# Later fetches of the raw channel weights, some scalings given to VectorE, and joined k-v products, in a fused attention and mixer kernel

## The chip, the cores and the metric

The kernel runs on one core of one Trainium2 chip. The metric is the device time of one execution in microseconds; of several runs the median counts. Engines are called by the names of the profile: PE is TensorE's matrix multiply, PEld its weight load, DVE is VectorE, ACT is ScalarE, POOL is GpSimd, SP is SyncE, which here only issues DMAs.

## The reference

Eight batches of 576 tokens go through a linear attention of 8 heads of 64, and then through an MLP mixer.

```python
kv = np.einsum('bhsd,bhse->bhde', k, v)
out = np.einsum('bhsd,bhde->bhse', q, kv)
rms = np.sqrt(np.mean(out * out, axis=-1, keepdims=True) + 1e-06)
x = out / rms * g_norm            # then (B, S, H*D): 8 x 576 x 512
h = np.maximum(xt @ w_tok1, 0.0) @ w_tok2       # xt = x with tokens last
u = x + h.transpose(0, 2, 1)
h2 = np.maximum(u @ w_ch1, 0.0) @ w_ch2
out = u + h2
```

w_tok1 is 576 x 256, w_tok2 256 x 576, w_ch1 512 x 1536, w_ch2 1536 x 512. The four weights arrive as float64, q, k and v as float32.

## The kernel before, in words

**Pairs and stages.** Batches are taken two at a time, as four pairs. The program has an attention for each pair, and a token mixing for each pair, which turns the pair's x into u and writes it to DRAM (`u_dram`). They are played against each other: a stage holds the attention of one pair and the token mixing of the pair before. So there are five stages: "start" (attention of pair 0), "middle" (attention of pair 1, mixing of pair 0), two "steady" stages (attention of pairs 2 and 3, mixing of pairs 1 and 2), and "last" (mixing of pair 3). Then follows the channel mixing, three quarters of the span: group 0 by `channel1_once` and `channel2_once` (L619, L681), groups 1 to 8 by `channel1` and `channel2`, which are not touched.

**The order is written by hand.** Each stage is a list of strings of step names, and `play` (L1047) emits the steps in that order; `keep` holds every engine to it, so each engine executes its own steps in this order, and waits at a step until its inputs and its buffer are there. In the names, the first digit after the letters is mostly a chunk, c, and the second a half or a tile, t:

- `kv00`, `kv01`, `kv10`, `kv11`: the products of k and v of side 0 or 1 (a batch of the pair), for one half of the heads: 20 matmuls, which the profile counts as 40 (`kv`, L319). PE takes every fp32 matmul here as two instructions. `e00` and so on copy the result from PSUM (ps_kv, two buffers) to SBUF (kvp); outside the start this is ACT's.
- `a0` to `a3`, `a4`: the attend products of q and kvp for one chunk of tokens (a4: the remainder of both sides), into two PSUM banks ps_o, of which there are only two (`attend`, L359; `attend_rem`, L373). After each come two `g` (x = ps_o times the gain, DVE, L399) and two `q` (squares, ACT, L403), which free the banks. a0 and a1 read the q of side 0, a2 and a3 that of side 1, a4 both.
- `t` sums the squares (DVE, L420), `m`, `r`, `i` make the inverse root for a group of chunks (DVE, ACT, DVE).
- `s` scales a tile of x, 128 x 512, by the inverse root on ACT, as 8 instructions, one for each head (`scale`, L448); `p` does it whole on POOL (`scale_pool`, L455).
- `h00` to `h11` and `hr`: the first token product, of 512 columns, into PSUM ps_h; hr also makes h1 by four relus on ACT. `u0` to `u8`: the second token product, into ps_u; u then adds x on DVE, or, where a seed `z` has put x into the bank before (ACT, `z2`, `z4`, `z6`), ACT copies it out. u writes its tiles to `u_dram` by POOL's queue.
- `l00` and so on fetch k and v of the next pair, `lq0` and `lq1` its q; all on SP's queue. A q buffer is free when the attends of its side are done: there are two.

**Rounding the channel weights.** The float64 weights are brought to float32 block by block: `block` (L180) gives a fetch (SP, into one of four raw buffers), a scale (two ACT instructions, L154 and L157), a clamp, a shift and an addition of 16-bit limbs (DVE, L160, L164, L169), which frees the raw buffer. Five blocks of token weights are worked off in the start by name (`w`). The fourteen channel blocks, 0 to 7 of w_ch1 (786 KB each) and 8 to 13 of w_ch2 (1049 KB, two DMAs each), come from `stream` (L1029): an iterator of single steps. A number in a stage's list takes as many steps from it. The fetches of blocks 0 to 3 stand in the lists as `f0` to `f3`; from then on the stream itself fetches block n + 4 with the shift of block n. What is left is woven into "last", with the four sums of w_ch1 blocks that the channel mixing needs (`mix_ch1`), the transposes of group 0 (`c0` to `c3`: `turn_blocks`, `fetch_t`, `fetch_u`) and, as `c4`, the sums of its uT.

Of the kernel before, what the change touches and what calls it, by code (L numbers as in the profile page):

```python
# [20 lines left out]
def kernel(  # L21
# [32 lines left out]
    nc = tc.nc  # L54
    P = 128
    B, S, DM = k.shape
    D = g_norm.shape[0]
# [7 lines left out]
    HP = H // 2  # L65
# [41 lines left out]
    def do(f, *a, **kw):  # L107
        return lambda: f(*a, **kw)
# [4 lines left out]
    keep = tc.keep_in_program_order  # L113
# [189 lines left out]
    X = {}  # L303
# [5 lines left out]
    def attention(pair, groups):  # L309
# [131 lines left out]
        def inv_of(c, t):  # L441

            inv = stats_of(c)[2]
            if whole:
                return inv[:, t].rearrange("p (k h) o -> p k h o", h=2)
            return inv[:, :, ts(t, HP)].rearrange("p h k o -> p k h o")

        def scale(c, t):  # L448
            x = X[pair, c][:, t].rearrange("p (k h d) -> p k h d", h=2, d=D)
            inv = inv_of(c, t)  # L450
            for k in range(HP):
                for h in range(2):
                    keep(nc.scalar.activation(x[:, k, h], x[:, k, h], AF.Copy, scale=inv[:, k, h]))  # L453

        def scale_pool(c, t):  # L455
            x = X[pair, c][:, t].rearrange("p (k h d) -> p k h d", h=2, d=D)
            keep(nc.gpsimd.tensor_mul(x, x, inv_of(c, t).to_broadcast([P, HP, 2, D])))

        steps = {}
# [5 lines left out]
        for c in range(5):  # L465
            if whole:
                steps |= {f"a{c}{t}": do(attend_tile, c, t) if c < 4 else attend_tile_rem
                          for t in range(parts(c))}
            else:
                steps[f"a{c}"] = do(attend, c) if c < 4 else attend_rem  # L470
            for h in range(parts(c)):
                steps |= {f"{n}{c}{h}": do(f, c, h) for n, f in zip("gqt", (gain, square, total))}
            for t in range(1 if c == 4 else 2):
                steps |= {f"{n}{c}{t}": do(f, c, t) for n, f in zip("sp", (scale, scale_pool))}
        for g in groups:
            steps |= {f"m{g[0]}": do(mean, g), f"r{g[0]}": do(sqrt, g), f"i{g[0]}": do(invert, g)}
        return steps
# [81 lines left out]
    blocks, blocks_dram = {}, {}  # L559
# [466 lines left out]
                fill[done]()  # L1026
                done += 1

    def stream(blocks, ahead=4):  # L1029

        def all_of(*fs):
            return do(lambda: [f() for f in fs])

        steps = [blocks[0][1]]
        for n in range(len(blocks)):
            first = list(blocks[n][2:])
            if n + 1 < len(blocks):  # L1040
                first[0] = all_of(first[0], blocks[n + 1][1])
            if n + ahead < len(blocks):
                first[1] = all_of(first[1], blocks[n + ahead][0])
            steps += first
        return iter(steps)

    def play(lines, after={}, **stages):  # L1047

        for name in " ".join(lines).split():
            if name.isdigit():
                for _ in range(int(name)):
                    next(stages["rounding"], lambda: None)()
            elif name[0] == "-":
                stages["before"][name[1:]]()
            else:
                next(stages[s][name] for s in ("attention", "mixing", "more")
                     if name in stages.get(s, ()))()
# [26 lines left out]
    for block in tok1[2:] + tok2:  # L1086
# [5 lines left out]


    start = [
        "kv00 e00 l00 j14 w01 w11 w02 w03 w04 w12 w13 w14", "kv01 j10 e01 l01 f0",
        "a00 g00 q00", "a01 g01 q01 t00", "a10 g10 q10 t01 m0 r0", "a11 g11 q11 t10 i0 p00 p01",
        "kv10 j6 t11 m1 r1 e10 i1 s10 p11", "kv11 j2 e11", "h000 h001 h002 h003", "a20 g20 q20", "a21 g21 q21 t20",
        "h010 t21 m2 r2", "a30 g30 q30 i2 p20", "a31 g31 q31 t30", "h011 t31 m3 r3 p21", "a40 i3 p30 g40 q40 p31",
        "h012 h013 t40 m4 r4 w21 i4 s40 lq0 l10 l11"]
    middle = [  # L1100
        "kv00 e00 w31 w22 w23 w24", "h10 f1 -lq1 w32 w33 w34", "kv01 e01 w41 w42",
        "h11 f2 w43 w44", "hr l00 f3", "a0 q00 g01 q01 g00 t00 t01", "u0 z2 1", "u1 l01 1",
        "a1 q10 g11 q11 g10 t10 t11 m0 r0", "u2 i0", "kv10 e10 z4 s00", "u3 1 s01", "kv11 e11",
        "u4 1 z6", "a2 q20 g21 q21 g20 s10", "u5 t20 t21 1", "a4 q40 g41 q41 g40 lq0", "u6 t40 t41 1 l10",
        "a3 q30 g31 q31 g30 lq1 s11", "u7 t30 t31 m2 r2 1 i2 p20 p21 s30", "u8 1 l11 s31"]

    def steady(n0, n1):
        return [
            "kv00 e00 1 -s40", "h00 1", "kv01 e01 1", "h01 1", f"a0 q00 g01 q01 g00 l00 {n0}",
            "h10 t00 t01 1", "h11 l01 2", "hr 1 z2", "a1 q10 g11 q11 g10 1", "kv10 e10 t10 t11 m0 r0",  # L1110
            "u0 i0 1", "kv11 e11", "u1 1 s00 l10", "u2 z4", "a2 q20 g21 q21 g20", "u3 s01 t20 t21",
            "u4 z6 1 l11", "a4 q40 g41 q41 g40 lq0", "u5 s10 t40 t41 1", "a3 q30 g31 q31 g30 lq1",
            "u6 s11 t30 t31 m2 r2 i2 p20 p21 s30", f"u7 1 s31 {n1}", "u8 1"]

    attentions = [attention(0, ((0,), (1,), (2,), (3,), (4,)))]
    attentions += [attention(p, ((0, 1), (2, 3, 4))) for p in range(1, B // 2)]

    mixings = [token_mixing(p, (2, 4, 6)) for p in range(B // 2 - 1)]
    mixings.append(token_mixing(B // 2 - 1, range(2, 9), (0, 1)))
    more = {f"w{n}{k}": f for n, b in enumerate(tok1 + tok2) for k, f in enumerate(b)}  # L1120
    more |= {f"f{n}": b[0] for n, b in enumerate(channel)}
    rounding = stream(channel)

    def keep_warm(n):

        o = ps["h"].tile([P, DM], F32, name="ps_j", tag="h")
        for _ in range(n):
# [4 lines left out]
    play(middle, attention=attentions[1], mixing=mixings[0], before=attentions[0],  # L1132
         more=more, rounding=rounding)
    for n in range(1, B // 2 - 1):
        play(steady(*((1, 1), (0, 0))[n - 1]), attention=attentions[n + 1], mixing=mixings[n], before=attentions[n],
             rounding=rounding)


    left.close()
# [4 lines left out]
    first = ExitStack()  # L1144
# [7 lines left out]
    def turn(i):  # L1152
# [4 lines left out]
            fetch_u(0, i // 2)  # L1157

    last = [
        "h00 c0 2 -s40 2", "h01 c1 2", "h10 c2 2", "h11 c3 2", "hr z2 1", "u0 z3 1", "u1 z4 1", "u2 z5",  # L1160
        "u3 z6 1", "u4 z7 1", "u5 z8 1", "u6 1", "u7 c4", "u8"]
    more = {f"c{i}": do(turn, i) for i in range(J)}
    more[f"c{J}"] = lambda: [f() for f in outer_u(0)]
# [28 lines left out]
    n = len(sums1) // 3  # L1192
# [61 lines left out]
```

## Time and profile before

| | us |
|---|---|
| median of 3 runs | 807.58 (806.7 to 808.29) |
| the profiled execution, its time | 809.79 |
| its span, first to last instruction | 808.0 |
| PE busy | 789.6 (98%) |
| DVE busy | 638.8 (79%) |
| ACT busy | 316.1 (39%) |
| POOL busy | 92.7 (11%) |
| HBM read / written | 137.79 / 36.57 MB |

A PE that is busy in the page isn't at its peak: the ends of matmuls are modelled, and waits shorter than a matmul's pipeline hide in them. Times between the starts of weight loads or of groups of matmuls tell more. The mean granted clock of the core was 0.998. The profile's times are of one execution and are counted from its first instruction.

### The profile page before, as it was taken

What the parts mean: (1) busy time and instruction counts of PE and PEld (TensorE: products, weight loads), DVE (VectorE), ACT (ScalarE), POOL (GpSimd) and SP (SyncE); (2) the same over time, 40 slices, a digit from 0 to 9 for tenths busy, and PEclk for the clock granted to TensorE, in tenths of its full rate; (3) what the DMA queues carried; (4) which work ended last, traced back from release to release, by engine and by line L of the source; (5) the groups of instructions that cost most, each with busy time, mean ns of one, the idle gap of its engine ahead of it and who ended that gap; (6) DMA issues with size and microseconds to landing.
All of it is one profiled execution on the core that took longest, in us unless ns stands there. A gap on an engine that the chain in (4) does not pass through costs nothing.

```text
span 808.0 us, 17626 instructions
## 1 busy us (share of the span) xinstructions
PE 789.6 (98%) x7008; PEld 694.4 (86%) x7008; DVE 638.8 (79%) x1251; ACT 316.1 (39%) x857; POOL 92.7 (11%) x95
## 2 busy tenths in 40 slices
PE   6999998999999999999999999999999999999997
PEld 6655544544888899999999999999999999999997
DVE  2667577584786978978987997997897898799687
ACT  2377787664120134234234234332423423423331
POOL 1211111021000021012003003001101200300300
PEclk9999999999999999999999999999999999999999
DMA  9999999328258477468457648738736845763642
GB/s 291 321 358 338 343 331 364 119 92 261 102 175 296 170 243 232 135 214 271 146 203 238 197 156 257 231 118 270 256 121 218 265 158 192 240 199 125 216 147 82
DMA packets 95041, 175.50 MB, mean 217 GB/s; under 512 B 7024, under 2 KB 54128, under 8 KB 94960
## 3 DMA queue, kind: packets, MB, share of 16 engines
q1 hardware_dynamic: 90656, 163.21, 62.4%
q0 software_dynamic: 2624, 9.44, 3.0%
q10 hardware_dynamic: 1680, 1.74, 0.7%
q8 instruction: 55, 0.90, 0.4%
q14 instruction: 26, 0.21, 0.1%
HBM read 137.79 MB, written 36.57 MB: 216 GB/s over the span
## 4 chain that ended last, share of the span: by engine, by line
PE 84%; DVE 5%; DMA 5%; ACT 4%; SPq 1%; issue 1%; DVEq 0%; ACTq 0%
PE ps_a L128 36%; PE ps_b L128 18%; PE ps_c L128 9%; PE ps_u L128 6%; PE ps_h L128 6%; PE ps_v L128 3%; PE ps_w L128 2%; PE ps_o L128 2%; ACT x L453 2%; DMA qT<-in_q_dram 1%; DMA raw<-in_moe_w_tok_dram 1%; DMA xt<-u_dram 1%; PE ps_kv L128 1%; SPq L116 1%; DVE uT L119 1%
## 5 line engine op out<-in xcount | busy, mean ns | idle before, releaser
L119 POOL TENSOR_TENSOR v<-v,v 128x384 f32<-128x384 f32 (+1 forms) x48 | 61.4, 1300 | 504.7 <-ACT v L125 463.8
L125 ACT COPY u<-ps_a 128x128 f32<-128x128 f32 (+1 forms) x160 | 56.2, 351 | 157.8 <-PE ps_a L128 157.8
L128 PE MATMUL ps_b<-uT,sums 128*128 128x128 f32 x672 | 86.2, 276 | 0.0
L128 PEld LDWEIGHTS ps_b<-uT,sums 128*128 128x128 f32 x672 | 80.7, 192 | 0.2
L119 DVE TENSOR_TENSOR v<-v,v 128x768 f32<-128x768 f32 (+1 forms) x86 | 79.5, 932 | 1.1
L128 PE MATMUL ps_a<-uT,w_ch 128*128 128x128 f32 x576 | 79.0, 276 | 0.4 <-DVE u L119 0.4
L125 ACT COPY ps_c<-ps_a 128x128 f32<-128x128 f32 (+1 forms) x80 | 26.9, 336 | 129.2 <-PE ps_a L128 97.6
L128 PEld LDWEIGHTS ps_a<-uT,w_ch 128*128 128x128 f32 x576 | 71.4, 192 | 1.0 <-DVE u L119 0.8
L119 DVE TENSOR_TENSOR v<-ps_b,u 128x384 f32<-128x384 f32 x112 | 61.6, 550 | 12.6 <-PE ps_b L128 10.8
L119 DVE TENSOR_TENSOR uT<-uT 128x512 f32<-128x512 f32 (+4 forms) x103 | 63.1, 629 | 6.6 <-DMA uT<-blocks 5.8
L128 PE MATMUL ps_h<-x,w_tok 128*128 128x512 f32 (+1 forms) x160 | 67.7, 616 | 0.1
L128 PE MATMUL ps_u<-h,w_tok 128*128 128x512 f32 (+1 forms) x160 | 67.2, 606 | 0.0
L128 PE MATMUL ps_a<-uT,w 128*128 128x128 f32 x432 | 60.0, 275 | 0.0
L128 PEld LDWEIGHTS ps_h<-x,w_tok 128*128 128x128 f32 (+1 forms) x160 | 26.5, 193 | 32.4 <-issue 29.6
L128 PEld LDWEIGHTS ps_a<-uT,w 128*128 128x128 f32 x432 | 54.0, 192 | 0.0
L399 DVE TENSOR_TENSOR x<-ps_o,g_sb 128x512 f32<-128x512 f32 x32 | 21.8, 688 | 39.1 <-PE ps_o L128 31.7
L119 DVE TENSOR_TENSOR sv<-v 128x384 f32<-128x384 f32 x80 | 43.4, 551 | 9.8 <-ACT v L122 9.8
L122 ACT ACTIVATE v<-v 128x384 f32<-128x384 f32 (+1 forms) x86 | 42.6, 528 | 21.4 <-DVE v L119 20.9
L119 DVE TENSOR_TENSOR xg<-xg,r 128x512 f32<-128x512 f32 x74 | 50.0, 686 | 0.7
L128 PEld LDWEIGHTS ps_u<-h,w_tok 128*128 128x128 f32 (+1 forms) x160 | 24.8, 179 | 29.2 <-issue 25.9
L453 ACT ACTIVATE x<-x,inv 128x64 f32<-128x64 f32 x184 | 46.1, 340 | 6.4 <-DVE inv L439 6.4
L128 PE MATMUL ps_a<-uT,sums 128*128 128x128 f32 x336 | 46.9, 276 | 0.2 <-ACT ps_c L125 0.2
(130 smaller groups left out, 1582.8 us busy)
## 6 DMA issues: line engine op xcount, KB each, us to landing
sums<-sums SPq DMA_DIRECT2D x112, 576.0 KB, 4.1
qT<-in_q_dram SPq DMA_DIRECT2D x8, 1152.0 KB, 9.9
xt<-u_dram SPq DMA_DIRECT2D x36, 256.0 KB, 3.9
blocks<-y SPq DMA_DIRECT2D x72, 128.0 KB, 2.9
uT<-blocks SPq DMA_DIRECT2D x36, 256.0 KB, 4.8
xg<-u_dram SPq DMA_DIRECT2D x18, 512.0 KB, 5.5
k_in<-in_k_dram SPq DMA_DIRECT2D x16, 512.0 KB, 9.2
u_dram<-x POOLq DMA_DIRECT2D x16, 512.0 KB, 6.4
```

What stands on the lines that cost most here:

```text
L116: keep(engine.dma_start(o, i))
L119: keep(engine.tensor_tensor(out=o, in0=a, in1=b, op=op))
L122: keep(nc.scalar.activation(o, a, AF.Relu))
L125: keep(nc.scalar.copy(o, a))
L128: keep(nc.tensor.matmul(*a, **kw))
L399: keep(nc.vector.tensor_mul(x, bank[c, h], g_sb.to_broadcast([P, number(c), D])))
L453: keep(nc.scalar.activation(x[:, k, h], x[:, k, h], AF.Copy, scale=inv[:, k, h]))
```

## The change

It does four things. (1) The fetches of all channel blocks get places of their own in the lists: f0 leaves the start, f0 to f2 stand in the middle, f3 to f7 in the first steady stage, f8 to f13 in the second, whose attention fetches no further k, v or q; `stream` no longer fetches. (2) The lists take fewer steps from the stream, and the scale of the next block moves from the clamp to the shift of the one before. (3) A new step `d` scales a tile whole by DVE; in the steady stages d00, d11, d20, d31 and d40 take the place of s00, s11, p20, s31 and s40, in the middle d00, d11 and d31; in the steady stages s01 and s10 move up. (4) In the steady stages kv00 and kv01 follow each other, and so do kv10 and kv11. Of the diff, the lists of the middle and the steady stages are given whole.

```diff
--- before.py
+++ after.py
@@ -452,6 +452,10 @@
                 for h in range(2):
                     keep(nc.scalar.activation(x[:, k, h], x[:, k, h], AF.Copy, scale=inv[:, k, h]))

+        def scale_vector(c, t):
+            x = X[pair, c][:, t].rearrange("p (k h d) -> p k h d", h=2, d=D)
+            keep(nc.vector.tensor_mul(x, x, inv_of(c, t).to_broadcast([P, HP, 2, D])))
+
         def scale_pool(c, t):
             x = X[pair, c][:, t].rearrange("p (k h d) -> p k h d", h=2, d=D)
             keep(nc.gpsimd.tensor_mul(x, x, inv_of(c, t).to_broadcast([P, HP, 2, D])))
@@ -471,7 +475,7 @@
             for h in range(parts(c)):
                 steps |= {f"{n}{c}{h}": do(f, c, h) for n, f in zip("gqt", (gain, square, total))}
             for t in range(1 if c == 4 else 2):
-                steps |= {f"{n}{c}{t}": do(f, c, t) for n, f in zip("sp", (scale, scale_pool))}
+                steps |= {f"{n}{c}{t}": do(f, c, t) for n, f in zip("spd", (scale, scale_pool, scale_vector))}
         for g in groups:
             steps |= {f"m{g[0]}": do(mean, g), f"r{g[0]}": do(sqrt, g), f"i{g[0]}": do(invert, g)}
         return steps
@@ -1026,22 +1030,17 @@
                 fill[done]()
                 done += 1

-    def stream(blocks, ahead=4):
-
-
-
-
-        def all_of(*fs):
-            return do(lambda: [f() for f in fs])
+    def stream(blocks):
+
+        def both(f, g):
+            return lambda: (f(), g())

         steps = [blocks[0][1]]
         for n in range(len(blocks)):
-            first = list(blocks[n][2:])
+            clamp, shift, add = blocks[n][2:]
             if n + 1 < len(blocks):
-                first[0] = all_of(first[0], blocks[n + 1][1])
-            if n + ahead < len(blocks):
-                first[1] = all_of(first[1], blocks[n + ahead][0])
-            steps += first
+                shift = both(shift, blocks[n + 1][1])
+            steps += [clamp, shift, add]
         return iter(steps)

     def play(lines, after={}, **stages):
@@ -1092,25 +1091,28 @@


     start = [
-        "kv00 e00 l00 j14 w01 w11 w02 w03 w04 w12 w13 w14", "kv01 j10 e01 l01 f0",
+        "kv00 e00 l00 j14 w01 w11 w02 w03 w04 w12 w13 w14", "kv01 j10 e01 l01",
         "a00 g00 q00", "a01 g01 q01 t00", "a10 g10 q10 t01 m0 r0", "a11 g11 q11 t10 i0 p00 p01",
         "kv10 j6 t11 m1 r1 e10 i1 s10 p11", "kv11 j2 e11", "h000 h001 h002 h003", "a20 g20 q20", "a21 g21 q21 t20",
         "h010 t21 m2 r2", "a30 g30 q30 i2 p20", "a31 g31 q31 t30", "h011 t31 m3 r3 p21", "a40 i3 p30 g40 q40 p31",
         "h012 h013 t40 m4 r4 w21 i4 s40 lq0 l10 l11"]
     middle = [
-        "kv00 e00 w31 w22 w23 w24", "h10 f1 -lq1 w32 w33 w34", "kv01 e01 w41 w42",
-        "h11 f2 w43 w44", "hr l00 f3", "a0 q00 g01 q01 g00 t00 t01", "u0 z2 1", "u1 l01 1",
-        "a1 q10 g11 q11 g10 t10 t11 m0 r0", "u2 i0", "kv10 e10 z4 s00", "u3 1 s01", "kv11 e11",
-        "u4 1 z6", "a2 q20 g21 q21 g20 s10", "u5 t20 t21 1", "a4 q40 g41 q41 g40 lq0", "u6 t40 t41 1 l10",
-        "a3 q30 g31 q31 g30 lq1 s11", "u7 t30 t31 m2 r2 1 i2 p20 p21 s30", "u8 1 l11 s31"]
-
-    def steady(n0, n1):
-        return [
-            "kv00 e00 1 -s40", "h00 1", "kv01 e01 1", "h01 1", f"a0 q00 g01 q01 g00 l00 {n0}",
-            "h10 t00 t01 1", "h11 l01 2", "hr 1 z2", "a1 q10 g11 q11 g10 1", "kv10 e10 t10 t11 m0 r0",
-            "u0 i0 1", "kv11 e11", "u1 1 s00 l10", "u2 z4", "a2 q20 g21 q21 g20", "u3 s01 t20 t21",
-            "u4 z6 1 l11", "a4 q40 g41 q41 g40 lq0", "u5 s10 t40 t41 1", "a3 q30 g31 q31 g30 lq1",
-            "u6 s11 t30 t31 m2 r2 i2 p20 p21 s30", f"u7 1 s31 {n1}", "u8 1"]
+        "kv00 e00 w31 w22 w23 w24", "h10 -lq1 w32 w33 w34", "kv01 e01 w41 w42",
+        "h11 w43 w44", "hr l00", "a0 q00 g01 q01 g00 t00 t01", "u0 z2 f0", "u1 l01",
+        "a1 q10 g11 q11 g10 t10 t11 m0 r0", "u2 i0", "kv10 e10 z4 d00", "u3 s01", "kv11 e11",
+        "u4 z6 f1", "a2 q20 g21 q21 g20 s10", "u5 t20 t21 1 f2", "a4 q40 g41 q41 g40 lq0", "u6 t40 t41 1 l10",
+        "a3 q30 g31 q31 g30 lq1 d11", "u7 t30 t31 m2 r2 1 i2 p20 p21 s30", "u8 1 l11 d31"]
+    steady = [[
+        "kv00 kv01 e00 e01 1 -d40 f3", "h00 1", "h01 1 f4", "a0 q00 g01 q01 g00 l00 1",
+        "h10 t00 t01 1", "h11 l01 1", "hr 1 z2 f5 f6", "a1 q10 g11 q11 g10", "kv10 kv11 e10 e11 t10 t11 m0 r0",
+        "u0 i0 1", "u1 1 d00 l10", "u2 s01 z4 1 f7", "a2 q20 g21 q21 g20", "u3 s10 t20 t21",
+        "u4 z6 1 l11", "a4 q40 g41 q41 g40 lq0", "u5 d11 t40 t41 1", "a3 q30 g31 q31 g30 lq1",
+        "u6 t30 t31 m2 r2 i2 d20 p21 s30", "u7 1 d31 1", "u8 1"], [
+        "kv00 kv01 e00 e01 1 -d40 f8", "h00 1", "h01 1 f9", "a0 q00 g01 q01 g00",
+        "h10 t00 t01 1", "h11 1", "hr 1 z2 f10", "a1 q10 g11 q11 g10", "kv10 kv11 e10 e11 t10 t11 m0 r0",
+        "u0 i0 1", "u1 1 d00 f11", "u2 s01 z4 1", "a2 q20 g21 q21 g20", "u3 s10 t20 t21",
+        "u4 z6 1 f12", "a4 q40 g41 q41 g40", "u5 d11 t40 t41 1", "a3 q30 g31 q31 g30",
+        "u6 t30 t31 m2 r2 i2 d20 p21 s30", "u7 1 d31", "u8 f13"]]

     attentions = [attention(0, ((0,), (1,), (2,), (3,), (4,)))]
     attentions += [attention(p, ((0, 1), (2, 3, 4))) for p in range(1, B // 2)]
@@ -1132,8 +1134,8 @@
     play(middle, attention=attentions[1], mixing=mixings[0], before=attentions[0],
          more=more, rounding=rounding)
     for n in range(1, B // 2 - 1):
-        play(steady(*((1, 1), (0, 0))[n - 1]), attention=attentions[n + 1], mixing=mixings[n], before=attentions[n],
-             rounding=rounding)
+        play(steady[n - 1], attention=attentions[n + 1], mixing=mixings[n], before=attentions[n],
+             more=more, rounding=rounding)


     left.close()
@@ -1157,7 +1159,7 @@
             fetch_u(0, i // 2)

     last = [
-        "h00 c0 2 -s40 2", "h01 c1 2", "h10 c2 2", "h11 c3 2", "hr z2 1", "u0 z3 1", "u1 z4 1", "u2 z5",
+        "h00 c0 2 -d40 2", "h01 c1 2", "h10 c2 2", "h11 c3 2", "hr z2 1", "u0 z3 1", "u1 z4 1", "u2 z5",
         "u3 z6 1", "u4 z7 1", "u5 z8 1", "u6 1", "u7 c4", "u8"]
     more = {f"c{i}": do(turn, i) for i in range(J)}
     more[f"c{J}"] = lambda: [f() for f in outer_u(0)]
```

## The prediction

> **What bounds the kernel.** I read the page first: how busy the engines are, and the chain that ended last.
>
> ```profile
> PE 789.6 (98%) x7008; PEld 694.4 (86%) x7008; DVE 638.8 (79%) x1251; ACT 316.1 (39%) x857; POOL 92.7 (11%) x95
> ...
> PE 84%; DVE 5%; DMA 5%; ACT 4%; SPq 1%; issue 1%; DVEq 0%; ACTq 0%
> ```
>
> TensorE (PE) bounds it, so an edit is worth only what it takes out of, or puts between, matmuls. The weight loads show the four attention stages that the change touches: start to 40.2 us, "middle" 40.2 to 77.7, first steady stage to 121.1, second to 168.9, "last" to 200.6. The windows by stage:
>
> ```profile
> 40.00:77.70 37.70, 36.54 (x511) 19.46 (x512) 25.31 (x54) 29.18 (x79) 4.37 (x5) 1.00 1.05 359
> 77.70:121.10 43.40, 43.24 (x532) 22.53 (x530) 29.69 (x54) 32.54 (x94) 5.78 (x7) 1.00 1.00 328
> 121.10:168.90 47.80, 45.17 (x532) 22.98 (x528) 31.27 (x52) 36.46 (x93) 5.95 (x7) 0.96 0.61 221
> 168.90:200.60 31.70, 31.70 (x83) 13.21 (x81) 21.55 (x30) 15.67 (x45) 6.66 (x8) 1.00 0.60 183
> ```
>
> Both steady stages do the same matmuls, yet one takes 43.3 us and the other 47.85. The DMA share is full through the first 120 us. The timeline of PE names the hole:
>
> ```profile
> 122.75 3.70 PE L128 MATMUL ps_h<-x,w_tok 128*128 128x512 f32 x8
> 126.38 1.39 PE L128 MATMUL ps_kv<-v_in,k_in 128*64 128x64 f32 x40
> 127.69 3.70 PE L128 MATMUL ps_h<-x,w_tok 128*128 128x512 f32 x8
> 134.02 1.16 PE L128 MATMUL ps_o<-kvp,qT 64*64 64x64 f32 x64 [2.63 <-DMA qT<-in_q_dram]
> ```
>
> SP's queue shows why q is late. Its fetch is issued at 122.25 behind two raw-weight fetches, and lands 11.7 us later:
>
> ```profile
> 117.44 1.40 SPq L116 DMA_DIRECT2D raw<-in_moe_w_ch_dram  x2
> 118.94 1.98 SPq L116 DMA_DIRECT2D k_in<-in_k_dram  x2
> 120.97 1.18 SPq L116 DMA_DIRECT2D v_in<-in_v_dram  x2
> 122.25 1.47 SPq L116 DMA_DIRECT2D qT<-in_q_dram  x2
> 126.94 13.97 SPq L116 DMA_DIRECT2D raw<-in_moe_w_ch_dram  x6
> ```
>
> The raw fetch at 117.44 had to wait for VectorE (DVE): its buffer is freed by the limb addition (L169) four blocks back. The hole has an echo. The same 24 matmuls in the chain, first stage and second:
>
> ```profile
> 89.56 8.98 PE ps_h L128 x24
> ...
> 135.19 10.68 PE ps_h L128 x24
> ```
>
> and the granted clock after the hole:
>
> ```profile
> 134.00:140.00 6.00, 5.98 (x72) 3.15 (x73) 4.66 (x7) 2.48 (x4) 0.00 (x0) 0.72 1.04 385
> ```
>
> Last, ScalarE (ACT) in the middle stage, before its third full attend (a3):
>
> ```profile
> 68.53 0.60 ACT L403 ACTIVATE sq<-ps_o 128x512 f32<-128x512 f32 x1 [0.17 <-DVE x L399]
> 69.03 2.00 ACT L453 ACTIVATE x<-x,inv 128x64 f32<-128x64 f32 x8
> 70.94 0.90 ACT L154 ACTIVATE w_ch<-raw 128x768 f32<-128x768 f32 x1
> 71.73 0.89 ACT L157 ACTIVATE raw<-raw 128x768 uint32<-128x768 uint32 x1
> 72.51 0.64 ACT L403 ACTIVATE sq<-ps_r 128x256 f32<-128x256 f32 x2
> ```
>
> A scaling (2.0 us) and one block's decoding (1.6 us) stand ahead of the squares that free a4's ps_o banks. PE could have begun a3 at 72.1 (u6 at 70.18 plus 1.91); it began at 73.2. This 1.1 us is the price of such an order.
>
> **What the Trainium skill says.** "TensorE: Matmul & The Clock Gate", The HAM clock gate: a free-running window of 3413 ns in which PE is idle halves the clock for the next. The trace agrees, and shows that 2.6 us of wait can be enough: 0.72 of the clock over 6 us is 3.4 us at half speed, 1.7 us lost. The same page, Architectural detail: ACT's and DVE's queues are strict FIFO; the rows at 70.94 to 72.51 show it. "DMA: Bandwidth & Descriptors", Issuing engines are not separate DMA queues: all share 16 engines, so a fetch taken from ahead of q really frees q; the DMA share of 1.00 to 1.05 agrees.
>
> **The change, part by part.**
>
> (1) Fetches. The end of the first steady stage had issued raw blocks 0 to 11; now 0 to 7. Ahead of the stage's first q (block 10 was the last ahead of it), three blocks of 1.05 MB fall out, at 0.34 MB/us 9 us of traffic. No k, v or q has more ahead of it than before. SP is moved past as well: block 7's fetch waits for block 3's addition, placed one line earlier, so q issues once the remainder's attend (a4) ends, near 112, and should land by about 120. It is needed near 131. POOL's u_dram writes go by a queue of their own and share only the 16 engines. The wait of 2.63 us and the half-clock window go: **-4.4**. If the DMAs stay as slow as at 122 (11.7 us), it still lands in time.
>
> What the fetches now meet: block 13 stands on SP ahead of the last stage's first xt, and its buffer is freed by block 9's addition, which DVE reaches about 1.3 us into "last". Two issues (1.0) and a landing (3.9, xt row of part 6, plus some for the megabyte ahead) put xt at about 7 us; its transpose was at 5.6. So c0 starts 1.5 late. In the first steady stage block 3's fetch stands behind the middle's last q: by the bytes ahead of it, it lands near 91. ACT, in order, may stand at its decoding until then; behind it are the h1 relus, due at 98. Hidden.
>
> (2) Rounding. Middle and both steady stages made 39 DVE steps; now 30. Nine steps (7.8 us of DVE at 0.68 + 0.69 + 1.23 a block) and three decodings (2.1 us of ACT each) move into "last". There DVE was busy 21.6 of 31.7 us, with 4.8 and 8.8 us of idleness near the end. In order: c0 at 7.2; rounding and one scaling 4.0 more before c1; four weight sums of 1.7 with the transposes, so c3 ends near 20.8 instead of 18.1. uT then lands 2.7 later, at 27.7 and 29.5 (25.0 and 26.8 before). Eight steps, two more additions and the sums of uT follow on DVE: the sum that channel1's second product needs is ready near 30.6. That product issues at 33.3. Cost **0**; the cover is 2.7 us, and behind it PE has 1.2 us of wait at 207.4 (16 matmuls in 4.62, elsewhere 3.45). Beyond both each us costs one. Bounds 0 to +2.
>
> (3) Scalings. Per steady stage ACT sheds four of seven (8 us) and POOL one of two (1.13 each); DVE gets five. The trace shows no such DVE multiply; the nearest row, xg<-xg,r of the same 128x512 from SBUF, is 0.69, so 3.4 us a stage (POOL's row would make it 5.7). In a steady stage 2 or 3 rounding steps leave (1.2 to 2.6 us): DVE near 33 of 43. Cost 0, behind the matmuls. Gain: the middle stage's a2 waited for kvp's copy behind 3.93 us of scalings (66.49, a2 at 66.2): **-0.35**; likewise the first steady a0, 1.48 instead of 1.09: **-0.4**. The middle's a3 keeps its 1.1: its scaling and its decoding stay where they were.
>
> New waits. Each steady stage now puts s01 ahead of z4 and of a2's squares, where it stood behind them. Take a2's start as 0. u2's copy ends at 0.8, s01 at 2.7, z4 at 3.2, while u4's first matmul is due at 2.95: **0.3**. In the first steady stage block 5's decoding is placed at u4, ahead of a4's squares: squares to 4.2, s10 to 6.1, copy and z6 to 7.0, decoding to 8.6, square to 9.0, g40 to 9.45; a3 is due at 7.6. **+1.8**. In the second stage no decoding stands there: g40 ends near 7.95, **+0.3**. Together **+2.7**. Bounds: 0, if ACT reaches these steps earlier than I reckon, to +4.4, with a half-clock window behind the 1.8. A gain below 0 is excluded: these waits weren't there before.
>
> (4) Joined k-v products. Before, h8, kv40, h8 took 3.63 + 1.31 + 3.63. A run of n matmuls of 512 columns takes 0.43 n + 0.19 (8: 3.63; 4: 1.91), 40 more k-v weight loads at a spacing of (1.25 - 0.14)/39 = 0.0285 take 1.14: joined, 7.07 + 1.14 in place of 8.57 saves 0.36. The same at u0. Four joins: **-1.4** (-1.0 if only the gaps between runs go, 0.19 + 0.06 each). The two ps_kv buffers hold both halves; the copies come before a0 and a2 by 7 and 5 us of matmuls.
>
> Sum: -4.4 - 0.35 - 0.4 - 1.4 + 2.7 = -3.85. The profiled execution took 809.79 us, its span 808.0, so 805.9; the three runs' median is 2.2 below that execution, so **803.7**.
>
> **The rivals.**
>
> (A) The forecast, 803.7: q on time, joins real, a3 delayed by ACT. For it: the same order cost 1.1 us at 72 us. Chance 0.5.
>
> (B) ACT is early enough, all four waits vanish: 807.6 - 6.55 = 801.0. For it: ACT had 32.5 busy us of 43.4, and loses 8. Against: its order, not its load, makes the wait. 0.24.
>
> (C) The new wait halves the clock for one window (+1.7, 805.4), or part of the q wait stays (2 us of it, 805.7): in all 805.3 to 808. For it: 1.8 us of idleness next to small attends is near what sufficed at 134. Against: 1.1 us at 72 did nothing. 0.18.
>
> (D) Slower: DVE, near full in "last", falls behind, and channel1's first products wait for uT. Place: xt behind block 13 on SP, then 16 steps woven among the transposes. It costs nothing up to 3.9 us of slip, then 1 us each; the kernel is slower than before from 7.7 us of slip, and 10 give 809.8. For it: DVE would have some 32 us of work and waits in 31.7. Against: the slip that I count is 2.7. 0.08.
>
> That the change doesn't do what it says is part of (C).
>
> **How the numbers follow.** Measurement can tell about 0.2% from no change, 806.0 to 809.2. A, B and two fifths of C lie below: 0.8 with rounding. Same: most of the rest of C, 0.13. Slower: D, 0.07. The range of 800.8 to 806.6 holds B, A and most of C; D, C's upper part and a better case than B stay outside, about 2 in 10.
>
> **What would show it.** No PE wait for qT, the 24 ps_h matmuls near 8.98 in both stages, clock 1.00: step 1. Two ps_kv runs of 80 and one of 16 ps_h: step 4. ACT's squares of ps_r near 1.8 us past a3's due time in the first steady stage: step 3. "last" at 31.6 us and channel1's first products without a wait for uT: step 2. A long wait of DVE for xt or uT near 175 to 200, or a wait of ps_v on uT, would make the prediction wrong; so would a second dip of the clock.

## The result and the profile after

| | us |
|---|---|
| changed kernel, first four runs | 806.81 (805.79 to 807.7) |
| kernel before, four runs beside it | 807.93 |
| ratio, 95% interval | 0.9988 [0.9968, 1.0008] |
| changed kernel, 22 later runs | 806.42 |
| kernel before, 55 runs beside those | 807.42 |
| ratio, 95% interval | 0.9986 [0.9978, 0.9995] |
| profiled executions, before and after | 809.79 and 805.97 |

The change is worth about 1.1 us (0.4 to 1.8, from the second interval), where 3.9 were forecast. The two profiled executions, though, lie 3.82 apart, and the sum of the prediction was 3.85; the four stages end at 196.76 instead of 200.56. So the sum fits the step between these two executions, and not the step between the medians. Why is the question of what follows.

Busy times of the changed kernel and the chain that ended last:

```profile
PE 784.7 (98%) x7008; PEld 692.2 (86%) x7008; DVE 645.0 (80%) x1265; ACT 294.3 (37%) x761; POOL 91.3 (11%) x93
...
PE 89%; DMA 4%; DVE 3%; ACT 2%; issue 1%; SPq 0%; ACTq 0%; DVEq 0%
```

ACT shed 22 us and DVE took on 6; PE is still 98% busy, so again only what lies between matmuls counts. The windows of the four stages (the middle one, the two steady ones, "last"), after:

```profile
40.16:77.33 37.17, 36.14 (x511) 19.37 (x512) 23.98 (x51) 22.75 (x59) 4.38 (x5) 1.00 1.02 332
77.33:121.69 44.36, 42.77 (x531) 22.51 (x529) 30.80 (x58) 25.47 (x61) 6.20 (x7) 1.00 1.06 357
121.69:165.02 43.33, 43.21 (x532) 22.50 (x528) 30.81 (x58) 26.55 (x60) 5.04 (x6) 1.00 0.59 213
165.02:196.76 31.74, 31.74 (x82) 13.08 (x80) 28.73 (x38) 17.42 (x31) 5.76 (x7) 1.00 0.68 209
```

The second steady stage lost 4.5 us and the clock there is 1.00; the first one became a microsecond longer. PE's timeline at the second one's start, after:

```profile
122.12 2.50 PE L128 MATMUL ps_kv<-v_in,k_in 128*64 128x64 f32 x80
124.55 7.13 PE L128 MATMUL ps_h<-x,w_tok 128*128 128x512 f32 x16
131.61 1.16 PE L128 MATMUL ps_o<-kvp,qT 64*64 64x64 f32 x64
132.70 9.05 PE L128 MATMUL ps_h<-x,w_tok 128*128 128x512 f32 x24
```

The k-v products stand in one run of 80, nothing waits for q, and the 24 matmuls are back at 9.05. SP's queue, after:

```profile
107.09 1.39 SPq L116 DMA_DIRECT2D k_in<-in_k_dram  x2
108.53 1.74 SPq L116 DMA_DIRECT2D v_in<-in_v_dram  x2
112.08 5.15 SPq L116 DMA_DIRECT2D qT<-in_q_dram  x2
118.36 35.41 SPq L116 DMA_DIRECT2D raw<-in_moe_w_ch_dram  x10
153.94 0.97 SPq L116 DMA_DIRECT2D xt<-u_dram  x2
167.98 1.32 SPq L116 DMA_DIRECT2D raw<-in_moe_w_ch_dram  x2
```

The pair of q fetches begins at 112.08, as reckoned, and a first pair of xt fetches stands ahead of block 13's raw fetch, not behind it, as the prediction had read from the list. And PE's timeline in the first steady stage, after:

```profile
107.34 4.09 PE L128 MATMUL ps_u<-h,w_tok 128*128 128x512 f32 x8
111.36 0.69 PE L128 MATMUL ps_r<-kvp,qT 64*64 64x64 f32 x32
111.99 1.98 PE L128 MATMUL ps_u<-h,w_tok 128*128 128x512 f32 x4
115.44 1.35 PE L128 MATMUL ps_o<-kvp,qT 64*64 64x64 f32 x64 [1.47 <-ACT sq L403]
```

The same place in the first profile of before:

```profile
108.83 3.70 PE L128 MATMUL ps_u<-h,w_tok 128*128 128x512 f32 x8
113.08 1.98 PE L128 MATMUL ps_u<-h,w_tok 128*128 128x512 f32 x4
115.00 1.16 PE L128 MATMUL ps_o<-kvp,qT 64*64 64x64 f32 x64
```

a3 waits for ACT's squares, and the eight matmuls ahead of a4 take 4.09 instead of 3.70: the two new waits that were forecast (1.8 and 0.3).

### The profile page after: what moved, and what is told of

Read it like the earlier page. It is cut to its first block, busy times and chain, and to the rows that moved or that the text cites. A ratio compares the mean times of both kernels' runs of the same rounds, so it can differ in the third digit from the quotient of the medians.

```text
span 803.9 us, 17541 instructions
## 1 busy us (share of the span) xinstructions
PE 784.7 (98%) x7008; PEld 692.2 (86%) x7008; DVE 645.0 (80%) x1265; ACT 294.3 (37%) x761; POOL 91.3 (11%) x93
## 4 chain that ended last, share of the span: by engine, by line
PE 89%; DMA 4%; DVE 3%; ACT 2%; issue 1%; SPq 0%; ACTq 0%; DVEq 0%
PE ps_a L128 37%; PE ps_b L128 19%; PE ps_c L128 10%; PE ps_h L128 8%; PE ps_u L128 7%; PE ps_v L128 3%; PE ps_kv L128 2%; DMA v_in<-in_v_dram 2%; PE ps_w L128 2%; PE ps_o L128 2%; ACT x L453 1%; DMA k_in<-in_k_dram 1%; DMA sums<-sums 1%; DVE uT L119 1%; DVE sv L119 1%
## 5 line engine op out<-in xcount | busy, mean ns | idle before, releaser
L128 PE MATMUL ps_h<-x,w_tok 128*128 128x512 f32 (+1 forms) x160 | 65.4, 603 | 0.0
L119 DVE TENSOR_TENSOR sv<-v 128x384 f32<-128x384 f32 x80 | 43.3, 550 | 8.8 <-ACT v L122 8.8
L128 PE MATMUL ps_a<-sums,sv 128*128 128x128 f32 x336 | 47.0, 276 | 0.0
```

The costliest lines, as they stand in the source:

```text
L119: keep(engine.tensor_tensor(out=o, in0=a, in1=b, op=op))
L128: keep(nc.tensor.matmul(*a, **kw))
```

## Experiments

**The theories.** T1: the edits do inside the stages what the sum said, and the missing part lies in the kernel before. Its half-clock window (1.7 us of the 4.4) is no fixed property of it but comes in some executions, so that the median never held it whole. T2: part of the gain is given back later, in "last" (the decodings and rounding steps moved there) or in the channel mixing. T3: the joins, or the scalings, gain less than reckoned.

**before_again**: the kernel before, unedited, with a second profile.

> The kernel before, unchanged, profiled a second time. Theory U (the profiled execution of before was an uncommon one): the first attend of the second steady stage waits less than 2.6 us for q, and the half-speed window of 3.4 us behind it is missing; the stages up to channel1's first product end 1 to 3 us earlier than 200.6 us, and the timed ratio is 1.000. Theory G (the gain is there in every execution and is given back later): wait and half-speed window are as in the first profile, stages end at 200.6 +/- 0.4 us.

22 runs: 806.91, ratio 0.9992 [0.9981, 1.0003] against 55 other runs of the same kernel. The second profile's span is 805.1, not 808.0. PE's timeline and the six microseconds after the wait:

```profile
133.63 1.16 PE L128 MATMUL ps_o<-kvp,qT 64*64 64x64 f32 x64 [2.57 <-DMA qT<-in_q_dram]
134.72 9.05 PE L128 MATMUL ps_h<-x,w_tok 128*128 128x512 f32 x24
```

```profile
134.00:140.00 6.00, 6.00 (x68) 3.06 (x59) 5.04 (x7) 2.50 (x4) 0.00 (x0) 1.00 1.03 378
```

The wait is nearly the same (2.57 against 2.63), but the clock stays at 1.00 and the 24 matmuls take 9.05, not 10.7. The second steady stage lasts 46.1 us here, 47.85 in the first profile. So T1 holds as far as this: the window isn't in every execution.

**before_third**: the kernel before once more.

> The kernel before, third profile: with a half-speed window behind the wait for q (second steady stage 47.8 us) or without it (46.1 us), about one to one; the wait itself 2.5 to 3.1 us in either case.

Time 806.71, span 804.9, and no half-clock window again. The wait is there (waits of PE, second steady stage):

```profile
PE ps_o L128 <- DMA qT<-in_q_dram: 2.3, 1, 2.3
```

One in three profiles of this kernel shows the window. The runs' mean granted clock says more: over three batches, 69 of 134 runs of the kernel before have a mean of 0.997 or less, with a median time of 807.97; the other 65 have 806.64, and the median of all is 807.57. The division is rough: a window lowers the mean by 3.4 x 0.5 / 808 = 0.002, and the kernel's start and end lower it as well by amounts that vary (the profile with the window has 0.998, before_third 0.998 without it). It suggests that about half of the executions have the window, and that it lifts the median by some 0.9 us.

**after_again**: the changed kernel once more.

> The changed kernel, unchanged, profiled a second time. Its four runs so far stood in two pairs, 805.8 to 806.0 and 807.65 to 807.7 us. Theory U: the attention stages end at 196.8 +/- 0.4 us again, the channel mixing takes 607.1 +/- 0.5 us, and what divides the pairs is at the start or in waits of 1 to 2 us that come and go in both kernels; ratio 0.996 to 1.000. Theory G: the part after 200 us is 1.5 to 3 us longer than that of before in most executions.

806.42 (22 runs), the ratio given above; span 804.0. Only 1 of 22 runs has a mean clock of 0.997 or less, though a3's wait of 1.5 us is in it.

**seed_first**: whatever its name says, this is the changed kernel a third time, with no edit.

> The changed kernel once more, for one look: attention stages end at 196.8 to 197.2 us, the last stage 31.7 to 32.2 us against 31.65 of before.

Time 806.34, span 804.5. Its last stage is 32.15, longer than the 31.74 and 31.98 of the other two profiles: PE waits there 0.2 us for ACT's seeding copy into ps_u.

**filled_wait**: the kernel before, with PE kept busy through most of the wait for q: nine matmuls of the identity, results unused, ahead of the second steady stage's a0 (there `warm` is "jk").

```diff
+def fill_wait():
+    o = ps["kv"].tile([P, 2, P], F32, name="ps_k", tag="kv")
+    for _ in range(9):
+        matmul(o[:, 0], lhsT=ident, rhs=ident, start=True, stop=True)
+
+more["jk"] = fill_wait
...
-"kv01 e01 1", "h01 1",
+"kv01 e01 1", f"h01 1 {warm}",
```

> The kernel before with nine matmuls of the identity (2.0 us of PE, results unused) put ahead of the first attend of the second steady stage, into the wait for q. They can't shorten the wait, only fill it. If the half-speed window behind the wait is what made the profiled execution of before uncommonly slow, and comes in a part of the executions, the window doesn't come: the median falls by the window's share, 0.5 to 1.2 us (ratio 0.9985 to 0.9994), and the second steady stage lasts 46.1 us, not 47.85. If the window is no part of it: ratio 1.000 or more.

806.51 (22 runs), 0.9988 [0.9979, 0.9997]; no run has a mean clock of 0.997 or less, against 19 of the 36 runs of the kernel before beside it, and 6 of 22 in before_again. The stage lasts 46.15. PE's timeline:

```profile
127.10 3.70 PE L128 MATMUL ps_h<-x,w_tok 128*128 128x512 f32 x8
130.63 2.17 PE L128 MATMUL ps_k<-ident 128*128 128x128 f32 x18
133.42 1.16 PE L128 MATMUL ps_o<-kvp,qT 64*64 64x64 f32 x64 [0.61 <-DMA qT<-in_q_dram]
134.51 9.05 PE L128 MATMUL ps_h<-x,w_tok 128*128 128x512 f32 x24
```

Counted from the stage's start, a0 begins no earlier than in before_again (12.96 us against 12.91); the filling only keeps PE active, and q comes when it comes. The kernel gains 1.0 us (0.2 to 1.7) from it, much as the two groups of runs suggest (0.9) and as half of 1.7 would. The changed kernel has no window either, and no wait for q; it should be ahead of this one by what is left of the sum without the window, 3.85 - 1.7 = 2.15 us. By the two ratios it is ahead by 807.42 x (0.9988 - 0.9986) = 0.2 us, uncertain by about 1 us (an estimate from the two intervals). So a part of what the stages gain doesn't reach the time of the kernel.

**order**: the changed kernel with the scalings put later (s01 from u2 to u3, s10 from u3 to u5), and block 5's decoding moved from u4 to u5, behind a4's squares.

```diff
-"u2 s01 z4 1 f7", ... "u3 s10 t20 t21", "u4 z6 1 l11", ... "u5 d11 t40 t41 1"
+"u2 z4 1 f7", ... "u3 s01 t20 t21", "u4 z6 l11", ... "u5 1 s10 d11 t40 t41 1"
...
-"u2 s01 z4 1", ... "u3 s10 t20 t21", ... "u5 d11 t40 t41 1"
+"u2 z4 1", ... "u3 s01 t20 t21", ... "u5 s10 d11 t40 t41 1"
```

> The changed kernel with the three ACT steps put back behind the squares: s01 at u3, s10 at u5, and block 5's decoding (with its shift) at u5 instead of u4. If ACT's order is what delays PE in the steady stages, the waits of 0.39 us at u4 in both stages and of 1.54 us at a3 in the first vanish: 2.3 us less than the changed kernel, ratio to before about 0.9955 to 0.996. If these waits come from ACT's load, at least 1 us of them stays.

805.08 (10 runs), 0.9969 [0.9953, 0.9985], span 801.7. The two steady stages last 42.24 and 42.76 instead of 44.36 and 43.33: 2.7 us, what the prediction gave for the new waits. Against the changed kernel the median falls by 1.3 only, since "last" grows from 31.74 to 32.95. PE's line there, and ACT's:

```profile
186.41 9.00 PE L128 MATMUL ps_u<-h,w_tok 128*128 128x512 f32 x24 [1.04 <-ACT ps_u L125]
```

```profile
183.66 1.18 ACT L154 ACTIVATE w_ch<-raw 128x1024 f32<-128x1024 f32 x1 [2.75 <-DVE w_ch L169]
```

ACT has reached block 13's decoding (L154) too early. It stands 2.75 us for DVE's limb addition (L169), which frees the block's buffer, and the seed z4 that PE needs is queued behind it. Here part of the gain is given back in "last": T2.

**fetch_only**: parts 1 and 2 alone; all scalings (`d` back to `s` and `p`) and the k-v products (`"kv00 e00 1", "h00 1", "kv01 e01", "h01 1"`) as before.

> The kernel before with the fetch places and the later rounding steps alone; scalings on ACT and POOL as before, k-v products apart. My sum gives this part the q wait with its half-speed window: no wait of a0 for q, second steady stage near 43.4 us instead of 47.85. Against the median of before: theory U, 0 to 2.5 us faster (ratio 0.997 to 1.000); theory G, 4.4 us faster (0.9945), less about 2 us if block 5's decoding, now ahead of a4's squares, delays a3 without the other scalings moved.

808.68 (14 runs), 1.0009 [0.9997, 1.0021], span 807.4. The q wait is gone and the second steady stage takes 43.6 us, yet nothing is gained. The first steady stage takes 44.0 us instead of 43.3, since block 5's decoding alone, with s01 and s10 in their old places, makes a3 wait 0.8 us. The larger loss is in "last". PE and ACT there:

```profile
180.72 7.13 PE L128 MATMUL ps_u<-h,w_tok 128*128 128x512 f32 x16
190.89 10.70 PE L128 MATMUL ps_u<-h,w_tok 128*128 128x512 f32 x24 [3.04 <-ACT ps_u L125]
```

```profile
182.27 1.12 ACT L125 COPY ps_u<-x 128x512 f32<-128x512 f32 x2
188.18 1.15 ACT L154 ACTIVATE w_ch<-raw 128x1024 f32<-128x1024 f32 x1 [4.79 <-DVE w_ch L169]
189.21 1.14 ACT L157 ACTIVATE raw<-raw 128x1024 uint32<-128x1024 uint32 x1
190.24 0.60 ACT L125 COPY ps_u<-x 128x512 f32<-128x512 f32 x1
```

The same place as in order, and far worse: 3.04 us of wait and a half-clock window behind it (10.70 for 24 matmuls), and "last" takes 36.65 instead of 31.65. The wait for q is gone, and one for a seed has come, with the same echo. 9 of these 14 runs have a mean clock of 0.997 or less. DVE's own lateness begins at its first weight sum:

```profile
178.00 1.76 DVE L119 TENSOR_TENSOR w<-w_ch 128x1536 f32<-128x1536 f32 x1 [4.06 <-DMA u_dram<-x]
```

It waits for the last write to `u_dram`, which takes 7.7 us to land; the DMA engines are full meanwhile (1.03 of their time from 174 to 178 us), with block 13's fetch among the traffic. In the changed kernel this wait is 0.67 us. How far the fetch is the cause was not tried.

**fetch_seed**: fetch_only with z4 put ahead of block 13's decoding.

```diff
-"hr z2 1", "u0 z3 1", "u1 z4 1", "u2 z5",
+"hr z2 1", "u0 z3", "u1 z4 1", "u2 z5 1",
```

> The run with fetch places and rounding steps alone, and in the last stage block 13's decoding put behind the seed z4 instead of ahead of it. If that order is what made its last stage 36.6 us long instead of 31.65 (z4 standing on ACT behind a decoding that waits for DVE), the wait of u4 for z4 (3.0 us) and the half-speed window behind it vanish: last stage 31.7 to 32.5 us, median 4 us below the run without it, near 804.5, ratio 0.996. If the wait moves on to z5 or to the sums of uT, the last stage stays above 33 us.

807.18 (13 runs), 1.0002 [0.999, 1.0013], span 804.8. "last" falls by 2.9, but to 33.71 only, not to the stage of before:

```profile
191.41 7.29 PE L128 MATMUL ps_u<-h,w_tok 128*128 128x512 f32 x20 [1.80 <-ACT ps_u L125]
```

```profile
188.22 1.17 ACT L154 ACTIVATE w_ch<-raw 128x1024 f32<-128x1024 f32 x1 [4.27 <-DVE w_ch L169]
```

The decoding stands nearly as long, and the next seed, z5, is now the one behind it. So the order on ACT is a part of the loss, and behind it stands DVE's addition, which is as late as before: DVE's wait for `u_dram` is 4.07 us here too.

**after_seed**: the changed kernel with the same edit.

> The changed kernel with that one mending alone (z4 ahead of block 13's decoding in the last stage). Its last stage took 31.7 to 32.15 us in three profiles, 31.65 in the kernel before. If the order costs that, 31.65 us again: 0.1 to 0.5 us less, ratio 0.998.

805.92 (21 runs), 0.9981 [0.9973, 0.9989], span 803.4, "last" 31.65. Beside the changed kernel's 0.9986 the intervals overlap; the stage shows the 0.1 to 0.5 us that "last" had lost.

**join_only**: the kernel before with the k-v products joined, nothing else.

```diff
-"kv00 e00 1 -s40", "h00 1", "kv01 e01 1", "h01 1"
+"kv00 kv01 e00 e01 1 -s40", "h00 1", "1", "h01 1"
...
-"kv10 e10 t10 t11 m0 r0", "u0 i0 1", "kv11 e11", "u1 1 s00 l10"
+"kv10 kv11 e10 e11 t10 t11 m0 r0", "u0 i0 1", "u1 1 s00 l10"
```

> The kernel before with the k-v products of the steady stages joined and nothing else. My sum: 0.36 us at each of four places, 1.4 us, less what the wait for q takes back in the second stage, where PE only arrives earlier at it: first stage 0.7 us shorter, second stage 0.4 us shorter after the wait and 0 before it; about 1.1 us in all, ratio 0.9987.

806.74 (14 runs), 0.9994 [0.9982, 1.0007]. From the starts of its groups, a join takes 2.86 + 7.06 = 9.92 where before_again has 1.69 + 3.63 + 1.31 + 3.63 = 10.26: 0.34 saved, and 0.34 at u0, against 0.36 forecast. The first steady stage is 1.0 us shorter (42.35), as a0 no longer waits there for kvp's copy, which now stands ahead of a scaling on ACT. But the second steady stage can't keep its first join:

```profile
PE ps_o L128 <- DMA qT<-in_q_dram: 3.1, 1, 3.1
```

PE is earlier and q is not, so the wait grows. The half-clock window is there too in this profile, and 10 of 14 runs are at 0.997 or less. These 10 aren't the slower ones, though (median 806.49; the other four 807.37), which shows how rough the mark is. The joins are real, but the one ahead of q's wait only together with part 1.

**scale_only**: the kernel before with DVE's scalings in the places of the old ones.

> The kernel before with the five scalings of a steady stage and three of the middle given to DVE, all at their old places; fetches, rounding steps and k-v products as before. My sum: a2 of the middle 0.35 us and a0 of the first steady stage 0.4 us earlier; in the second stage the wait for q takes back what is early. DVE stays below the matmuls. So 0 to 0.8 us faster, ratio 0.999 to 1.000. If DVE's added 3.4 us a stage delay the additions that free raw buffers, q comes later and the ratio is over 1.000.

807.94 (14 runs), 1.0008 [0.9997, 1.0019], span 804.5: no gain to be told. In the profile the waits ahead of the middle's a2 and the first steady a0 are gone (both 1.09), and q's wait remains:

```profile
PE ps_o L128 <- DMA qT<-in_q_dram: 2.5, 1, 2.5
```

Why its median isn't 0.4 to 0.7 lower was not found.

**all_orders**: order, the seed edit of after_seed, and the same cure in the middle stage.

```diff
-"a2 q20 g21 q21 g20 s10", "u5 t20 t21 1 f2", "a4 q40 g41 q41 g40 lq0", "u6 t40 t41 1 l10"
+"a2 q20 g21 q21 g20", "u5 t20 t21 f2", "a4 q40 g41 q41 g40 lq0 1", "u6 s10 t40 t41 1 l10"
```

> The changed kernel with ACT's order mended at four places: s01, s10 and block 5's decoding as in the run with the order mended; in the middle, s10 and block 0's decoding behind a4's squares; in the last stage the seed z4 ahead of block 13's decoding. If waits of PE for ACT's order are what is left to win: a3 of the middle no longer waits 1.1 us, u4 of the last stage no longer waits 1.0 us, 2.1 us less than with the first mending, and 4.7 us of the stages less than the changed kernel: median near 803, ratio 0.994 to 0.995. If ACT's load is the bound, the waits move to the next step on ACT.

803.29 (7 runs), 0.995 [0.9931, 0.9968]: faster than both kernels. The windows by stage:

```profile
40.13:76.33 36.20, 35.96 (x511) 19.19 (x512) 21.52 (x47) 22.21 (x59) 4.37 (x5) 1.00 1.01 332
76.33:118.57 42.24, 42.24 (x530) 22.41 (x528) 32.89 (x59) 25.91 (x62) 6.19 (x7) 1.00 1.07 363
118.57:161.34 42.77, 42.77 (x532) 22.41 (x529) 30.58 (x56) 26.88 (x61) 5.04 (x6) 1.00 0.65 236
161.34:192.99 31.65, 31.65 (x83) 13.16 (x81) 29.57 (x41) 17.33 (x31) 5.76 (x7) 1.00 0.65 203
```

PE's busy column now equals the stage in three of four and is 0.24 us short in the middle one; from there on, no wait of PE is longer than 0.5 us. The only edits against the changed kernel are steps in another order on ACT (and the rounding that goes with a decoding); by the two ratios (0.9986 and 0.995) they are worth 2.9 us, more than the change.

## Why the forecast was wrong

What it got right, stage by stage. The profile of before without a window (before_again) is set against the changed kernel's:

| stage | before_again | after | moved | forecast without the window |
|---|---|---|---|---|
| middle | 37.54 | 37.17 | -0.4 | -0.35 |
| first steady | 43.3 | 44.36 | +1.0 | -0.4 - 0.72 + 2.1 = +1.0 |
| second steady | 46.1 | 43.33 | -2.8 | -2.63 - 0.72 + 0.6 = -2.75 |
| last | 31.65 | 31.74 to 32.15 | +0.1 to +0.5 | 0 |

The signs that the prediction named for its steps came nearly as named: no wait for qT and a clock of 1.00, k-v runs of 80, a3 late by ACT's squares, "last" near 31.6 us. What failed is the way from the profiled execution to the median.

**(1) Fetches: the step that failed.** The wait for qT went, 2.6 us, as forecast. The half-clock window went as well, where there was one. The step reads "The wait of 2.63 us and the half-clock window go: -4.4". That is true of the profiled execution. The prediction then noted that the median lay 2.2 below that execution, and still took the whole 4.4 off the median, 1.7 of it for the window. A good part of those 2.2 was the window itself: by the runs' clocks it is in about half of the executions, and filled_wait and the two groups of runs put its worth for the median at 0.9 to 1.0. So this term was too large by 0.7 to 0.8. What could have warned me is in the prediction's own lines: an execution 2.2 above the median has something that most others lack, and the window was its one known oddity.

This is not the whole miss. Of 3.85 forecast, 1.1 came: 2.7 are missing. Besides the window, "last" took 0.1 to 0.5 (step 2), and the channel mixing, which the prediction put at nothing, was 0.4 to 0.7 longer than in the two profiles of before without a window. Together these are 1.2 to 2.0 us; the rest is open, and the 1.1 is itself uncertain by 0.7.

The detail on SP failed as well, without cost: c0 was to start 1.5 us late behind block 13. The first xt pair is ahead of it on the real queue, and c0 came 4.0 us into "last", earlier than the 5.6 of before.

**(2) Rounding: mechanism missed, size small.** I set 0 for what moves into "last", with uT as the place of danger. uT was never late. The loss lies on ACT: block 13's decoding waits for DVE's addition, and the seeds for PE stand behind it. In the changed kernel "last" is 0.1 to 0.5 us longer; with DVE or PE elsewhere in time the wait is 1.04 (order) or 3.04 and a window (fetch_only). after_seed and all_orders take it away, and the stage returns to 31.65.

**(3) Scalings.** DVE's multiply was put at 0.69; the group of L457, after (min, median, max in ns):

```profile
L457 DVE TENSOR_TENSOR x<-x,inv x14: 676/682/1541, 62.2 to 171.1; 128x512 f32<-128x512 f32 x14
```

-0.35 came (the stage table), and a0's -0.4 is seen in scale_only (1.48 to 1.09), and in join_only as well: either part alone takes that wait away; the new waits came too: u4 by 0.39 in each stage (0.3 forecast), u5 to a3 3.45 instead of 1.91 (+1.54, and a3 itself 1.28 instead of 1.09, against 1.8) and 0.18 in the second stage (0.3). ACT's timeline shows the order that does it:

```profile
106.90 2.02 ACT L453 ACTIVATE x<-x,inv 128x64 f32<-128x64 f32 x8
108.82 0.58 ACT L125 COPY ps_u<-x 128x512 f32<-128x512 f32 x1
109.33 1.06 ACT L403 ACTIVATE sq<-ps_o 128x512 f32<-128x512 f32 x2
110.29 2.01 ACT L453 ACTIVATE x<-x,inv 128x64 f32<-128x64 f32 x8
...
113.19 0.90 ACT L154 ACTIVATE w_ch<-raw 128x768 f32<-128x768 f32 x1
113.98 0.87 ACT L157 ACTIVATE raw<-raw 128x768 uint32<-128x768 uint32 x1
114.75 0.64 ACT L403 ACTIVATE sq<-ps_r 128x256 f32<-128x256 f32 x2
```

The squares of ps_r start at 114.75, behind a scaling and a decoding; a3 could have begun at 113.9. order confirmed it: with those steps later, 2.7 us leave the two stages.

**(4) Joins.** 0.34 each instead of 0.36.

**The rivals.** B fell: the new waits exist. C asked for a window behind the 1.8; there is none in three profiles, and 1 of 22 runs bears its mark. C's other arm, part of the q wait staying, did not happen. That the measured time lies within C's numbers (805.3 to 808) is therefore chance. D named uT, and uT was in time; its thought, that "last" would pay for DVE's load, came true in small and on another engine.

**What is not settled.** Without the window the forecast would be 2.15. The profiles without a window (before_again 805.1 and before_third 804.9 in span, against 803.9, 804.0 and 804.5) give 0.9; the runs with a mean clock above 0.997 (806.64 before, 806.37 in after_again) give 0.3. "last" explains up to 0.5 of what is missing there. The channel mixing that follows took 607.1 us in each of the changed kernel's three profiles and 607.46, 606.66 and 606.43 before. The changed one has a stop for the sums' fetch near 285 us,

```profile
PE ps_a L128 <- DMA sums<-sums: 1.0, 1, 1.0
```

(1.0, 0.84 and 0.34 in the three), which the kernel before doesn't have there, and 0.2 near 480 for DVE. The other profiles speak against laying this stop to the fetches or the rounding: filled_wait and scale_only, with the old fetch places, have it too (0.40 and 0.36 us), and fetch_only and fetch_seed, with the new ones, have none. In all_orders it is gone, and the mixing still takes 607.5. The mixing is the same program in every run here, and its length lies between 605.1 (join_only) and 607.5 us, so that differences of half a microsecond can't be laid to an edit by one profile each. Nor do the parts add up by their medians (fetch_only and scale_only above 1, join_only at 0.9994, all together 0.9986); the profiles say why for fetch_only and join_only, not for scale_only.

Nor is it settled why the window comes in one execution and not in another. In the profiles it stands behind the three longest waits and behind no shorter one (the last section has the numbers), so a difference of a tenth of a microsecond in the wait would be one explanation, and the place of the wait within a free-running window another. No run here separates them.

## What to carry to other kernels

A stall and its echo in the clock are two terms: here the stall was in every execution of the kernel before and the half-clock window in some, so look at several executions before the echo goes into a forecast of the median (their mean granted clock gives a rough mark). When a profiled execution is above the median, find what it has that the others lack, and count that part of the gain only as often as it comes. And a gain within stages is not yet a gain of the kernel: steps that wait in order on an engine hold up what stands behind them. In fetch_only a wait for q of 2.6 us was traded for one of 3.0 for a seed, and putting ACT's steps in another order was worth more (2.9 us) than the whole change (1.1).

## What the runs showed of the hardware

- A single wait of PE can halve its clock for 3.4 us. It did so behind waits of 2.63, 3.04 and 3.13 us (first profile of before, fetch_only, join_only) and not behind 2.57, 2.55 and 2.34 us (before_again, scale_only, before_third), nor behind 1.80 and 1.47 us (fetch_seed, after). The Trainium skill ("TensorE: Matmul & The Clock Gate", The HAM clock gate) gives a free-running window of 3413 ns and puts the halving after at least one idle window of about 3.4 us. The length of the half-clock stretch agrees; the waits here are all shorter than a whole window, and 2.63 us was enough once.
- With nine unused matmuls in the wait, 2.2 us, none of 22 runs had a mean clock of 0.997 or less, and 0.61 us of wait were left (filled_wait).
- DVE scales a tile of 128x512 in one instruction of 0.68 us (median); ACT needs eight of 128x64, 2.0 us in all.
